# Two more chunks transposed by the DMA crossbar, and the chunk blocks chained earlier, in a retention + gated feed-forward kernel

## Chip, cores, metric

One core of a Trainium2 chip. The metric is device time in microseconds (us) of one execution. All executions compared here carry the label "fast" (the label leaves in a few that were somewhat disturbed, such as one execution of the kernel before with 236.82 us at a granted clock of 0.991). A ratio is the mean time of one kernel's fast runs over the mean of the other's in the same rounds, so it is not quite the ratio of the medians quoted beside it.

## The reference, cut to what matters

```python
# q, k, v: (4 batches, 8 heads, 768 positions, 64), fp32
for t in range(S):                                   # retention, per batch and head
    state = gamma * state + outer(k[t], v[t])
    y[t]  = q[t] @ state / sqrt(64)
x = y as (3072 tokens, 512)
out = (sigmoid(x @ w_gate) * (x @ w_val)) @ w_out    # d_ff 1536
```

## The kernel before

The kernel cuts each batch into six chunks of 128 positions: 24 chunks, in six tiles of 512 tokens (four chunks each). A tile's feed-forward ("up" groups, then "down" groups) is one long stream of matmuls. The retention work of later chunks is put between its groups by a plan: `(group, step, chunks)`. The helpers that the change touches:

```python
def transposes(g):                       # TensorE: 8 transposes, then a copy out of PSUM on ScalarE
    tp = bank([128, 2 * NP, C], BF16)
    for i, x in enumerate((kn[g], qn[g])):
        for p in range(NP):
            nc.tensor.transpose(tp[:, i * NP + p, :], pair(x, p), ident)
    qkT[g] = at.tile(...)
    nc.scalar.activation(qkT[g], tp, AX.Copy)

def xbar(g):                             # the same by the DMA crossbar, two transfers from SyncE
    qkT[g] = ld.tile(...)
    for i, x in enumerate((kn[g], qn[g])):
        nc.sync.dma_start_transpose(out=qkT[g][:, i * NP:(i + 1) * NP, :], in_=...)

def step_t(g):  transposes(g); scale_v(g)            # scale_v: one multiplication on VectorE

def block(done, new):                    # outputs of two old chunks, scores of two new ones
    # TensorE: inter(olds), scores(news), intra(olds), state(news)
    # VectorE: y_out(olds), [state_sum if no olds], masks(news), [state_sum if olds]

def casts(g):                            # ScalarE: two casts per chunk, state to bf16
    for i in range(g, g + 2): ... state_out(i, za[i])
```

Chunks 12 to 23 already go by the crossbar. Chunks 4 to 11 are transposed on TensorE. The first tile ("t = 0") starts with groups already done in a prologue.

## Time and profile before

| | before |
|---|---|
| median, 3 runs | 234.52 us (234.31 to 234.71) |
| span of the profiled run | 232.9 us |
| TensorE busy | 223.6 us, 96% |
| VectorE, ScalarE busy | 119.4 and 90.2 us |
| first "down" matmul of the first tile | 39.43 us |
| last TensorE work | 228.80 us |

I use three lengths, read from the chain of waits. The **head** runs up to the first down piece of the first tile. The **stream** runs from there to the end of TensorE's last piece. The **tail** runs from there to the end of the span. Before: 39.43, 189.37 and 4.10 us. Pieces of the chain of the kernel before (columns: start, length, engine, tile, line, count):

```profile
39.43 2.59 PE ff L418 x12
...
53.15 0.88 PE ff L384 x8
...
93.34 3.45 PE ff L384 x16
...
226.14 2.66 PE ff L437 x36
```

The second tile begins at 53.15 and the third at 93.34.

### The profile page before, as it was taken

What the parts mean: (1) busy time and instruction counts of PE and PEld (TensorE: products, weight loads), DVE (VectorE), ACT (ScalarE), POOL (GpSimd) and SP (SyncE); (2) the same over time, 40 slices, a digit from 0 to 9 for tenths busy, and PEclk for the clock granted to TensorE, in tenths of its full rate; (3) what the DMA queues carried; (4) which work ended last, traced back from release to release, by engine and by line L of the source; (5) the groups of instructions that cost most, each with busy time, mean ns of one, the idle gap of its engine ahead of it and who ended that gap; (6) DMA issues with size and microseconds to landing.
All of it is one profiled execution on the core that took longest, in us unless ns stands there. A gap on an engine that the chain in (4) does not pass through costs nothing.

```text
span 232.9 us, 4615 instructions
## 1 busy us (share of the span) xinstructions
PE 223.6 (96%) x1882; PEld 124.7 (54%) x1882; DVE 119.4 (51%) x228; ACT 90.2 (39%) x165; POOL 75.5 (32%) x98
## 2 busy tenths in 40 slices
PE   4889999999999999999999999999999999999992
PEld 1557844568889644445445445445445454444452
DVE  5579344175986544476835367637267530334201
ACT  5865333545837221362611532613532412343220
POOL 7997756999863619026000000000000000000000
PEclk9999999999999999999999999999999999999999
DMA  7999999999999999989111442012100012100022
GB/s 136 184 225 196 199 206 211 238 235 258 217 150 127 161 136 238 259 133 166 49 45 64 119 91 47 0 45 79 61 0 3 0 46 90 48 0 0 1 90 93
DMA packets 73302, 27.05 MB, mean 116 GB/s; under 512 B 59840, under 2 KB 68928, under 8 KB 73280
## 3 DMA queue, kind: packets, MB, share of 16 engines
q0 software_dynamic: 55440, 16.78, 64.8%
q1 hardware_dynamic: 17696, 9.90, 19.5%
q8 instruction: 15, 0.25, 0.4%
q10 hardware_dynamic: 144, 0.07, 0.1%
q14 instruction: 7, 0.06, 0.1%
HBM read 28.31 MB, written 6.29 MB: 149 GB/s over the span
## 4 chain that ended last, share of the span: by engine, by line
PE 87%; DMA 3%; POOL 3%; DVE 2%; issue 2%; ACT 1%; POOLq 0%
PE ff L384 43%; PE ff L418 25%; PE ff L400 8%; DMA qr<-in_q_dram 3%; PE ff L233 2%; PE ff L184 2%; PE ff L196 2%; PE ff L163 1%; PE ff L437 1%; PE z L202 1%; POOL kr L77 1%; DVE stA L189 1%; ACT gs L388 1%; ACT zbd L208 0%; DVE xT L251 0%
## 5 line engine op out<-in xcount | busy, mean ns | idle before, releaser
L389 DVE TENSOR_TENSOR hT<-gs,ff 128x512 bf16<-128x512 f32 (+1 forms) x66 | 42.1, 646 | 58.7 <-PE ff L384 53.7
L384 PE MATMUL ff<-xT,wg 128*128 128x512 bf16 (+1 forms) x264 | 63.6, 363 | 0.0
L384 PE MATMUL ff<-xT,wv 128*128 128x512 bf16 (+1 forms) x264 | 63.5, 363 | 0.0
L418 PE MATMUL ff<-wo,hT 128*128 128x512 bf16 x276 | 62.3, 379 | 0.2 <-DVE hT L389 0.2
L388 ACT ACTIVATE gs<-ff 128x512 f32<-128x512 f32 (+1 forms) x66 | 37.2, 566 | 64.6 <-PE ff L384 57.5
L418 PEld LDWEIGHTS <-hT 128*128 128x128 bf16 x276 | 26.3, 98 | 31.2 <-DVE hT L389 0.6
L384 PEld LDWEIGHTS <-wv 128*128 128x128 bf16 x264 | 25.9, 98 | 26.9
L384 PEld LDWEIGHTS <-wg 128*128 128x128 bf16 x264 | 25.0, 98 | 26.0 <-DVE xT L251 0.3
L423 ACT COPY ob<-ff 128x512 f32<-128x512 f32 x23 | 13.5, 587 | 48.8 <-PE ff L418 45.9
L251 DVE TENSOR_TENSOR xT<-ff,taby 128x512 bf16<-128x512 f32 x20 | 12.9, 686 | 21.0 <-PE ff L233 21.0
L67 POOL DMA_DIRECT2D kn<-in_k_dram x20 | 18.0, 901 | 15.3 <-DMA qkX<-qn 9.9
L62 POOL DMA_DIRECT2D vf<-in_v_dram x20 | 18.2, 912 | 12.0 <-DMA kn<-in_k_dram 5.4
L208 ACT CAST zbd<-za 64x256 bf16<-64x256 f32 x38 | 15.4, 405 | 9.5 <-DVE za L220 8.0
L68 POOL DMA_DIRECT2D qn<-in_q_dram x20 | 18.1, 903 | 2.9 <-DMA wo<-in_moe_w_out_dram 1.6
L175 DVE TENSOR_TENSOR vs<-vf,tabv 128x512 bf16<-128x512 f32 x20 | 13.5, 685 | 1.9 <-DMA vf<-in_v_dram 1.8
L189 DVE TENSOR_TENSOR stA<-ff,causal 128x512 bf16<-128x512 f32 x20 | 13.6, 682 | 0.0
L190 DVE TENSOR_TENSOR stB<-ff,causal 128x512 bf16<-128x512 f32 x20 | 13.6, 681 | 0.0
L400 PE MATMUL ff<-xT,wg 128*128 128x256 bf16 x88 | 11.6, 273 | 0.3 <-DVE xT L342 0.3
L400 PE MATMUL ff<-xT,wv 128*128 128x256 bf16 x88 | 11.6, 273 | 0.0
L407 DVE TENSOR_TENSOR hT<-gs,ff 128x512 bf16<-128x512 f32 x11 | 7.5, 687 | 7.3 <-PE ff L400 5.6
L400 PEld LDWEIGHTS <-wg 128*128 128x128 bf16 x88 | 8.4, 98 | 1.7 <-issue 0.6
L406 ACT ACTIVATE gs<-ff 128x512 f32<-128x512 f32 x11 | 6.5, 598 | 7.2 <-PE ff L400 7.2
(84 smaller groups left out, 160.6 us busy)
## 6 DMA issues: line engine op xcount, KB each, us to landing
out_dram<-ob SPq DMA_DIRECT2D x23, 256.0 KB, 2.0
vf<-in_v_dram POOLq DMA_DIRECT2D x20, 256.0 KB, 7.3
kn<-in_k_dram POOLq DMA_DIRECT2D x20, 128.0 KB, 7.3
qn<-in_q_dram POOLq DMA_DIRECT2D x20, 128.0 KB, 7.4
wg<-in_moe_w_gate_dram POOLq DMA_DIRECT2D x6, 256.0 KB, 8.9
wv<-in_moe_w_val_dram POOLq DMA_DIRECT2D x6, 256.0 KB, 9.4
wo<-in_moe_w_out_dram POOLq DMA_DIRECT2D x4, 384.0 KB, 11.3
vr<-in_v_dram SPq DMA_DIRECT2D x1, 512.0 KB, 4.3
```

The lines of the kernel that those rows point to most:

```text
L62: nc.gpsimd.dma_start(out=vf[g], in_=src(v, g))
L67: nc.gpsimd.dma_start(out=kn[g], in_=src(k, g))
L68: nc.gpsimd.dma_start(out=qn[g], in_=src(q, g))
L175: nc.vector.tensor_tensor(vs[g], vf[g], tabv[:, g % NCH, :].unsqueeze(2).to_broadcast([C, H, D]), op=ALU.mult)
L189: nc.vector.tensor_tensor(stA[g], sc[g][0], causal4, op=ALU.mult)
L190: nc.vector.tensor_tensor(stB[g], sc[g][1], causal4, op=ALU.mult)
L208: nc.scalar.copy(zbd[g % 4][half, :, half], z[half])
L384: nc.tensor.matmul(u[:, lo:hi], w[:, kk, n1 * 128:(n1 + 1) * 128], x_cols(t, kk, lo, hi), start=(kk == 0), stop=(kk == KT - 1))
L388: nc.scalar.activation(gs[:, lo:hi], ps[0][:, lo:hi], AX.Sigmoid)
L389: nc.vector.tensor_tensor(hT[t][:, n1, lo:hi], gs[:, lo:hi], ps[1][:, lo:hi], op=ALU.mult)
L400: nc.tensor.matmul(u[:, i * n:(i + 1) * n], w[:, kk, n1 * 128:(n1 + 1) * 128], x_cols(t, kk, lo, hi), start=(kk == 0 and (rows == 1 or i = ...
L418: nc.tensor.matmul(o, hT[t][:, n1, sm * 128:(sm + 1) * 128], wo[:, n1, :], start=(n1 == 0), stop=(n1 == NFF - 1))
```

## The change

Its intent: take the transposes of chunks 10 and 11 off TensorE. For that their crossbar transfers stand at the head of SyncE's work in the second tile. The retention blocks are chained and moved earlier, so that fewer half-wide up groups are needed. Two more output buffers are meant to keep ScalarE from waiting when stores stand behind crossbar transfers.

```diff
-    XBAR = 12
+    XBAR = 10
-        ob = ffn.tile([128, D_MODEL], F32, tag="ob", name="ob")
+        ob = ffn.tile([128, D_MODEL], F32, tag="ob", name="ob", bufs=5)
 plan:
-        0: [(7, step_t, 4), (9, step_t, 5), (10, block, None, 4), (10, casts, 4), (11, step_t, 6), (12, block, 4, None)],
-        1: [(0, step_t, 7), (2, block, None, 6), (3, step_t, 8), (4, casts, 6), (5, step_t, 9), (7, block, 6, 8),
-            (9, casts, 8), (11, step_t, 10), (13, step_t, 11), (15, block, 8, 10), (17, casts, 10), (20, block, 10, None),
-            (22, scale_v, 12), (23, scale_v, 13)],
-        2: [(1, block, None, 12), (3, casts, 12), ...
+        0: [(6, step_t, 4), (7, step_t, 5), (8, block, None, 4), (9, step_t, 6), (10, casts, 4), (10, step_t, 7),
+            (12, block, 4, 6), (13, step_t, 8)],
+        1: [(0, casts, 6), (1, step_t, 9), (3, block, 6, 8), (5, casts, 8), (7, scale_v, 10), (9, scale_v, 11),
+            (11, block, 8, 10), (13, casts, 10), (14, scale_v, 12), (15, scale_v, 13), (18, block, 10, 12),
+            (20, casts, 12)],
+        2: [(0, scale_v, 14), (1, scale_v, 15), (4, block, 12, 14), ...
 second tile, column halves:
-            groups[:10] = [... up(1, n1, 0, 256) for n1 in range(10)]
-            groups[10:10] = [... up_columns(1, range(n1, n1 + 2), 256, 512) for n1 in range(0, 10, 2)]
+            groups[:6] = [... up(1, n1, 0, 256) for n1 in range(6)]
+            groups[6:6] = [... up_columns(1, range(n1, n1 + 2), 256, 512) for n1 in range(0, 6, 2)]
 loop over groups:
+            if t == 1 and i == 0:
+                for g in range(XBAR, 12):
+                    xbar(g)
             if i == len(groups) - 9:
                 for g in range(4 * t + 8, 4 * t + 12):
-                    if XBAR <= g < NG:
+                    if 12 <= g < NG:
                         xbar(g)
```

More of the change, by code (lines that the diff above doesn't have):

```diff
@@ L531 @@
     plan = {
-        0: [(7, step_t, 4), (9, step_t, 5), (10, block, None, 4), (10, casts, 4), (11, step_t, 6), (12, block, 4, None)],
-        1: [(0, step_t, 7), (2, block, None, 6), (3, step_t, 8), (4, casts, 6), (5, step_t, 9), (7, block, 6, 8),
-            (9, casts, 8), (11, step_t, 10), (13, step_t, 11), (15, block, 8, 10), (17, casts, 10), (20, block, 10, None),
-            (22, scale_v, 12), (23, scale_v, 13)],
-        2: [(1, block, None, 12), (3, casts, 12), (4, scale_v, 14), (5, scale_v, 15), (7, block, 12, 14),
-            (9, casts, 14), (13, scale_v, 16), (14, scale_v, 17), (16, block, 14, 16), (18, casts, 16)],
+        0: [(6, step_t, 4), (7, step_t, 5), (8, block, None, 4), (9, step_t, 6), (10, casts, 4), (10, step_t, 7),
[3 more added lines that the diff above has]
+            (20, casts, 12)],
+        2: [(0, scale_v, 14), (1, scale_v, 15), (4, block, 12, 14), (6, casts, 14), (11, scale_v, 16),
+            (12, scale_v, 17), (16, block, 14, 16), (18, casts, 16)],
         3: [(3, scale_v, 18), (4, scale_v, 19), (6, block, 16, 18), (8, casts, 18), (12, scale_v, 20),
@@ L551 @@
         if t == 1:
-            groups[:10] = [lambda n1=n1: up(1, n1, 0, 256) for n1 in range(10)]
-            groups[10:10] = [lambda n1=n1: up_columns(1, range(n1, n1 + 2), 256, 512) for n1 in range(0, 10, 2)]
+            groups[:6] = [lambda n1=n1: up(1, n1, 0, 256) for n1 in range(6)]
+            groups[6:6] = [lambda n1=n1: up_columns(1, range(n1, n1 + 2), 256, 512) for n1 in range(0, 6, 2)]
             for g in range(12, 16):
```

## The prediction

> **What bounds the kernel now.** I read the page's busy table and slices first, then the chain of waits, then the timeline of the second tile (52.99 to 93.18 us), where the change works, and last the DMA issues there. The busy table and the slices come first because they tell which engine's time is the kernel's time:
>
> ```profile
> PE 223.6 (96%) x1882; PEld 124.7 (54%) x1882; DVE 119.4 (51%) x228; ACT 90.2 (39%) x165; POOL 75.5 (32%) x98
> ...
> PE   4889999999999999999999999999999999999992
> ...
> PEclk9999999999999999999999999999999999999999
> DMA  7999999999999999989111442012100012100022
> ```
>
> TensorE (PE) works in every slice after the third, at the full granted clock. VectorE (DVE) and ScalarE (ACT) are near half. The DMA engines are full until about slice 18 (some 105 us), then nearly idle. So the kernel is TensorE's own stream after the first 16.7 us, and a change pays what it takes off that stream or out of the small holes in it. The groups by shape say what is in it:
>
> ```profile
> L384 PE MATMUL ff<-xT,wg 128*128 128x512 bf16 x224 | 57.5, 379 | 0.0
> L384 PE MATMUL ff<-xT,wg 128*128 128x256 bf16 x40 | 6.0, 273 | 0.0
> L163 PE MATMUL ff<-ident,qn 128*128 128x128 bf16 x32 | 3.1, 219 | 0.0
> L163 PE MATMUL ff<-ident,kn 128*128 128x128 bf16 x32 | 3.1, 219 | 0.0
> ```
>
> The 219 ns of a transpose is its latency; what it costs is the pitch, read from the timeline and the chain: eight transposes advance the stream by 0.447 us, so 55.9 ns each; four matmuls 512 wide by 0.864 us, so 216.0 ns; four 256 wide by 0.437 us, so 109.3 ns. The chain of waits shows the second tile's holes, where it leaves TensorE for ScalarE:
>
> ```profile
> 58.13 0.46 PE ff L163 x8
> 58.59 0.02 issue
> 58.61 0.02 ACT qkT L165
> ...
> 59.53 0.38 ACT gs L388
> ...
> 61.90 0.60 ACT qkT L165
> ...
> 63.52 0.38 PE ff L184 x7
> ```
>
> ScalarE carries a 1.02 us copy out of PSUM for each transposed chunk, the sigmoids of half-wide groups, and four state casts of 0.4 us. Here they queue: TensorE waits at the block of chunks 6 to 9 for the copy of chunk 9.
>
> How large are the holes? The second tile takes 40.19 us between chain entries (53.15 to 93.34). Its work at the pitches above: 160 half-wide matmuls 17.49; 16 full ones of the up part 3.46; 48 of the down part at 215.7 ns 10.35; five transposed chunks 2.24; scores of six chunks at 0.275 each 1.65; states of five at 0.185, 0.92; inter of five at 0.224, 1.12; intra of six at 0.285, 1.71. Sum 38.94, so **1.25 us of holes**. The first tile's down stage by the same count has 0.22 us (two pieces of six matmuls take 1.40 instead of 1.29).
>
> [...]merging two 256-wide matmuls into one saves only some 2.6 ns. [...]a crossbar transpose lands in 2.4 us at 130 us, and in 8 to 10.6 us between 60 and 77 us among the loads. [...]the loads of chunk 17, issued at 69.6 and 70.4 us while transposes were queued, took 17.0 and 16.7 us, and those issued at 41 to 44 us beside no transpose took 5.9 to 6.4.
>
> **The change part by part.**
>
> 1. Transposes. Chunks 10 and 11 leave TensorE: 2 x 8 x 55.9 ns = **0.89 us** off the stream, all on the path. Also two copies of 1.02 us leave ScalarE, which costs nothing by itself.
>
> 2. Half-wide groups. Second-tile groups cut in column halves fall from 10 to 6. That turns 64 matmuls of 256 columns into 32 of 512: 64 x 109.3 - 32 x 216.0 = **0.08 us** saved.
>
> 3. Order. In the first tile the blocks are now chained (scores of chunks 6 and 7 in the same block as the outputs of 4 and 5), transposes of 7 and 8 move there from the second tile, and the block of 12 and 13 moves from the third tile to the end of the second. This moves work, and takes none away. Laying the order out at the trace's pitches, the second tile starts about 54.8 us instead of 52.99, with 1.8 us more done.
>
> 4. Holes after the change. First tile: the copies of chunks 4 to 7 fall among down matmuls, where ScalarE has one 0.59 us output copy per 2.6 us, so I expect near none (0.22 saved). Second tile: the casts of chunks 6 and 7 now wait for VectorE's sums, which stand behind two output multiplications (1.2 us) and four masks (2.4 us) of the chained block: about 57.0 us. The casts end near 58.3, then sigmoid, the copy of chunk 9 (to 59.6) and two sigmoids (to 60.4). TensorE reaches the block of 6 to 9 at about 58.9 and needs those: an estimated **1.3 us** of holes, the same size as the 1.25 before, moved. The hole of 0.15 us where the down stage waits for VectorE at 83.9 is inside that 1.25; three up groups now follow the block of 8 to 11 instead of two, so this one should go. Third tile, by the same count as above: 0.37 us of holes before, and I leave it. So holes before in the two tiles 1.47, after about 1.3: **0.15 us** saved.
>
> 5. Crossbar. The four new issues stand behind the first tile's fourth output (copied at about 55.0) and behind the loads of chunks 10 and 11, landed at 54.2, 55.7, 57.3 and 58.1 us. Four issues of 1.3 to 1.6 us from 55.4, landing 8 to 10 us later, spaced 2 us: the last about 70. The block that reads them starts near 73.5: margin **some 3 to 4 us**. Later transposes shift by about 4 us: chunk 13 from 75.4 to 79.5, wanted at about 86.5; chunk 15 from 86.8 to 91, wanted at about 102; the values of chunk 13 from 65.1 to 69, wanted at 81. All hidden.
>
> 6. Fifth output buffer. The first store of the second tile would be held in SyncE's order behind chunk 15's transposes, until about 82 us at my shift; its copy comes about 84. So it is an insurance, worth nothing if step 5 holds.
>
> Sum: 0.89 + 0.08 + 0.15 = 1.1 us. **Predicted 233.4 us**, 0.5% faster.
>
> **Rivals.** First: the crossbar lands too late. For it: the loads in that stretch already take 13 to 17 us when transposes are among them, and transposes among loads land up to 10.6 us after issue. Against: 3 to 4 us of margin. If the last transpose lands 3 us past its need, TensorE waits 3 us, less the gain of 1.1: 236 to 237 us. Second: the holes grow. [...]the chained block puts 4.4 us on VectorE in front of the casts; if each of the two chained blocks in the half-wide stretch costs 1 us more than I laid out, the gain is eaten: 234.5 to 235. Third: the holes close. If the chain of casts fits, all 1.47 us go as well as the 0.97 of removed work: 232.1. More can't be had, as everything else on the stream is unchanged, so the downside is longer than the upside.
>
> **Range and chances.** 232.2 to 235.0: the low end is nearly the third rival, the high end the second or a small form of the first. Two per cent is 4.7 us; faster by that is out of reach of the sum (2.5 us at most), so 0.01. Slower by it needs the first rival at 6 us of wait: 0.03. Within: 0.96.
>
> **What would show it.** Right: 16 fewer transposes on TensorE and 32 fewer matmuls; eight-transpose pieces unchanged at 0.45 us; the second tile starting near 54.8 and ending near 92; no wait of TensorE for a crossbar transpose; holes between 58.5 and 61 us with ScalarE in the chain. Wrong: TensorE waiting for the transposed chunk 10 or 11 at about 73 us (step 5), a lower total of holes by over 0.6 us (step 4), or a stall of the third tile on chunks 14 to 17, whose loads come later.

Passages that no trace of this case shows are cut from it where marked. No term of its sum is among them: 0.89 + 0.08 + 0.15 = 1.12 us, given as 1.1. The 215.7 ns of a down matmul is the trace's own: in the chain of the kernel before, 30 of them take 6.47 us. The 2.6 ns of a merge are 2 x 109.3 - 216.0 from its measured pitches.

## The result

231.88 us median (231.38 to 232.04, 4 runs). The kernel before had 234.42 us (233.78 to 234.71, 4 runs). The ratio is 0.9892, 95% interval 0.9866 to 0.9918. So the change is faster by 1.1%: "within 2%" as expected, but 1.5 us better than predicted and below the range of 232.2 to 235.0.

The page of the changed kernel, its busy table and slices:

```profile
PE 222.0 (97%) x1834; PEld 120.9 (53%) x1834; DVE 119.1 (52%) x226; ACT 88.1 (38%) x161; POOL 75.3 (33%) x98
...
PE   4989999999999999999999999999999999999994
...
DMA  7999999999999999999997342011100012100022
```

TensorE has 48 matmul instructions fewer (1882 to 1834): 16 transposes, and 64 narrow matmuls that became 32 wide ones. It still bounds the kernel. The DMA engines stay full some three slices longer. The groups of TensorE by shape, of the changed kernel:

```profile
L384 PE MATMUL ff<-xT,wg 128*128 128x512 bf16 x240 | 61.6, 379 | 0.0
...
L384 PE MATMUL ff<-xT,wg 128*128 128x256 bf16 x24 | 3.6, 273 | 0.0
...
L163 PE MATMUL ff<-ident,kn 128*128 128x128 bf16 x24 | 2.3, 219 | 0.0
L163 PE MATMUL ff<-ident,qn 128*128 128x128 bf16 x24 | 2.3, 219 | 0.0
```

The marks in its chain of waits:

```profile
38.63 1.29 PE ff L418 x6
...
54.05 1.75 PE ff L384 x16
...
92.30 8.63 PE ff L384 x40
...
224.07 2.66 PE ff L437 x36
```

Head 38.63, stream 226.73 - 38.63 = 188.10, tail 229.6 - 226.73 = 2.87. So the span fell by 3.3 us in this pair of profiles: 0.80 in the head, **1.27 in the stream**, 1.2 in the tail. My prediction had worked on the stream alone. There it said 1.1.

The hole that the prediction laid out in the second tile is there, at the place it named:

```profile
56.24 0.45 PE ff L384 x4
...
56.73 0.40 ACT zbd L208
...
57.15 0.41 ACT zbd L208
...
57.57 0.38 ACT gs L388
57.96 0.50 ACT qkT L165
...
58.76 0.68 ACT gs L388 x2
...
59.48 0.38 PE ff L184 x7
```

The chain leaves TensorE at 56.7, walks through the casts of chunks 6 and 7, a sigmoid, the copy of chunk 9 and two sigmoids, and returns at 59.5. The part of this in which TensorE lost time comes from the same count as before. The second tile takes 92.30 - 54.05 = 38.25 us. Its work at the prediction's pitches is 20.86 (96 half-wide and 48 full up matmuls) + 10.35 (down) + 0.45 (one transposed chunk) + 5.40 (scores, states, inter and intra) = 37.06. That leaves 1.19 us of holes.

Where did the head's and the tail's 2 us come from? The head holds no part of the change. In the tail, the landings of the last three stores differ. DMA issues after 226 us, kernel before (columns: transfer, queue, operation, count, KB, us from issue to landing):

```profile
q8 instruction: 1, 0.02, 0.6%
issues: line engine op xcount, KB each, median us to landing
out_dram<-ob SPq DMA_DIRECT2D x1, 256.0 KB, 4.2
out_dram<-ob SPq DMA_DIRECT2D x1, 128.0 KB, 3.3
out_dram<-ob ACTq DMA_DIRECT2D x1, 64.0 KB, 3.0
out_dram<-ob SPq DMA_DIRECT2D x1, 64.0 KB, 2.5
```

The same window of the changed kernel:

```profile
q14 instruction: 1, 0.01, 0.2%
...
out_dram<-ob SPq DMA_DIRECT2D x1, 128.0 KB, 1.7
out_dram<-ob ACTq DMA_DIRECT2D x1, 64.0 KB, 1.6
out_dram<-ob SPq DMA_DIRECT2D x1, 64.0 KB, 1.6
```

In the kernel before, one 16 KB packet of the queue q8 "instruction" stands beside the last stores. Its record runs from 228.08 to 229.41 us. In the changed kernel there is none (its q14 record is an 8 KB packet of another queue, and the landings are short beside it). Over the whole span the page counts 15 such packets before and 14 after. The listing of the built program has 3766 rows on TensorE before and 3670 after (each of the 1882 or 1834 matmuls has a weight load, and two rows are other instructions).

### The profile page after: what moved, and what is told of

The parts are those of the page before. It is cut to its first block, busy times and chain, and to the rows that moved or that the text cites. A ratio compares the mean times of both kernels' runs of the same rounds, so it can differ in the third digit from the quotient of the medians.

```text
span 229.6 us, 4530 instructions
## 1 busy us (share of the span) xinstructions
PE 222.0 (97%) x1834; PEld 120.9 (53%) x1834; DVE 119.1 (52%) x226; ACT 88.1 (38%) x161; POOL 75.3 (33%) x98
## 4 chain that ended last, share of the span: by engine, by line
PE 90%; POOL 3%; DMA 3%; ACT 1%; issue 1%; DVE 0%; POOLq 0%; ACTq 0%
PE ff L384 47%; PE ff L418 26%; PE ff L400 6%; DMA qr<-in_q_dram 3%; PE ff L233 2%; PE ff L184 2%; PE ff L196 2%; PE ff L163 1%; PE ff L437 1%; PE z L202 1%; POOL kr L77 1%; ACT gs L388 0%; POOL qr L77 0%; POOL vr L77 0%; POOL maskr L455 0%
## 5 line engine op out<-in xcount | busy, mean ns | idle before, releaser
L389 DVE TENSOR_TENSOR hT<-gs,ff 128x512 bf16<-128x512 f32 (+1 forms) x66 | 43.2, 662 | 58.9 <-PE ff L384 55.5
L384 PE MATMUL ff<-xT,wg 128*128 128x512 bf16 (+1 forms) x264 | 65.2, 369 | 0.0
L384 PE MATMUL ff<-xT,wv 128*128 128x512 bf16 (+1 forms) x264 | 65.2, 369 | 0.0
L388 ACT ACTIVATE gs<-ff 128x512 f32<-128x512 f32 (+1 forms) x66 | 38.0, 578 | 67.4 <-PE ff L384 61.4
L384 PEld LDWEIGHTS <-wg 128*128 128x128 bf16 x264 | 25.3, 98 | 27.5
L400 PE MATMUL ff<-xT,wg 128*128 128x256 bf16 x72 | 9.5, 273 | 0.3 <-DVE xT L342 0.3
L400 PE MATMUL ff<-xT,wv 128*128 128x256 bf16 x72 | 9.5, 273 | 0.0
L429 PE MATMUL ff<-ident 128*128 128x512 bf16 x18 | 6.3, 487 | 3.0 <-POOL ident masks.py:199 3.0
L407 DVE TENSOR_TENSOR hT<-gs,ff 128x512 bf16<-128x512 f32 x9 | 6.1, 684 | 5.0 <-PE ff L400 3.7
L406 ACT ACTIVATE gs<-ff 128x512 f32<-128x512 f32 x9 | 5.2, 596 | 6.5 <-PE ff L400 6.5
## 6 DMA issues: line engine op xcount, KB each, us to landing
kn<-in_k_dram POOLq DMA_DIRECT2D x20, 128.0 KB, 11.1
```

Of the source, the lines that this page charges most:

```text
L384: nc.tensor.matmul(u[:, lo:hi], w[:, kk, n1 * 128:(n1 + 1) * 128], x_cols(t, kk, lo, hi), start=(kk == 0), stop=(kk == KT - 1))
L388: nc.scalar.activation(gs[:, lo:hi], ps[0][:, lo:hi], AX.Sigmoid)
L389: nc.vector.tensor_tensor(hT[t][:, n1, lo:hi], gs[:, lo:hi], ps[1][:, lo:hi], op=ALU.mult)
L400: nc.tensor.matmul(u[:, i * n:(i + 1) * n], w[:, kk, n1 * 128:(n1 + 1) * 128], x_cols(t, kk, lo, hi), start=(kk == 0 and (rows == 1 or i = ...
```

## The experiments

All numbers of head, stream and tail are from each run's one profile (the span is read to 0.1 us, so a tail is good to about 0.05):

| run | rows on TensorE | head | stream | tail | median us | ratio to before (95%) |
|---|---|---|---|---|---|---|
| before (first profile) | 3766 | 39.43 | 189.37 | 4.10 | 234.42 | |
| after (first profile) | 3670 | 38.63 | 188.10 | 2.87 | 231.88 | 0.9892 (0.9866 to 0.9918) |
| before again | 3766 | 39.09 | 189.38 | 3.73 | 233.92 | 0.9979 (0.9953 to 1.0004) |
| after again | 3670 | 39.57 | 188.11 | 2.92 | 232.30 | 0.9910 (0.9876 to 0.9944) |
| order only | 3702 | 38.84 | 188.99 | 3.17 | 233.21 | 0.9956 (0.9926 to 0.9986) |
| crossbar only | 3734 | 39.16 | 188.49 | 2.85 | 232.23 | 0.9914 (0.9872 to 0.9955) |
| five buffers only | 3766 | 38.89 | 189.37 | 3.74 | 234.16 | 1.0013 (0.9951 to 1.0074) |
| after, rows added | 3766 | 39.40 | 188.11 | 3.99 | 232.88 | 0.9943 (0.9903 to 0.9984) |
| before, rows added | 3878 | 39.35 | 189.37 | 3.18 | 233.20 | 0.9956 (0.9915 to 0.9996) |
| after, three buffers | 3670 | 39.22 | 188.11 | 2.87 | 231.96 | 0.9902 (0.9853 to 0.9951) |
| split casts | 3670 | 38.99 | 187.25 | 2.86 | 231.02 | 0.9872 (0.9846 to 0.9899) |
| split casts, early sums | 3670 | 38.74 | 187.01 | 3.15 | 230.68 | 0.9854 (0.9825 to 0.9882) |

The stream repeats to 0.01 us for the same order of work. The head wanders between 38.6 and 39.6 us, as the two repeats show: 39.09 for before, 39.57 for after.

### The two kernels again

No edit.

> The kernel before, unchanged, as a control. In the two profiles the changed kernel gains 1.27 us between the first TensorE piece of the steady stream (16.72 before, 15.93 after) and the last (228.81, 226.73); 0.79 us more came before it (landing of the query load) and 1.2 us after it (landing of the last stores). Theory A, chance at the ends: this control's ratio is 1.000, but its own profile shows a start and a tail that differ from the first profile by several tenths of a us, and can show the short ones (start near 15.9, tail near 2.9 us). Theory B, the change shortens both ends: start stays near 16.7 and tail near 4.1 here.

> The changed kernel, unchanged. Theory A: ratio near (234.4-1.3)/234.4 = 0.9945 on the same chip, about 1.3 us, with start and tail no different from the control's. Theory B: ratio again near 0.989 (2.5 us), start near 15.9 and tail near 2.9.

Before gave 233.92 us and 0.9979. So 0.2% (0.5 us between the medians) is what the same kernel can differ from itself, and the intervals are to be read with that. After gave 232.30 us and 0.9910. Neither theory held as written. The streams repeat, 189.38 and 188.11. The head is chance: after had the longest head of all here. But the tail is not chance, with 3.73 again for before and 2.92 again for after.

### Order only

```diff
 changed kernel:
-    XBAR = 10
+    XBAR = 12
-            (7, scale_v, 10), (9, scale_v, 11),
+            (7, step_t, 10), (9, step_t, 11),
```

> The changed order, split and five buffers, but chunks 10 and 11 transposed on TensorE in the places of their scalings. If my sum is right (0.89 us of transposes, 0.08 of half-wide pairs, the rest in holes), this loses 0.9 us to the changed kernel plus what two extra copies on ScalarE cost in holes: 0.3 to 0.5 us faster than before, ratio about 0.998. If the order is what matters (rival), it keeps most of the gain: ratio 0.994 or below.

The stream is 188.99, so 0.38 us shorter than before, in the 0.3 to 0.5 expected. It loses 0.89 us to the changed kernel, which is 16 transposes at 55.9 ns. The total (0.9956, some 1.0 us) is larger than the stream explains. It lies between the 0.998 expected and the rival's 0.994, and its interval holds both, so by time alone neither was decided. The tail, at 3.17, is short here too.

### Crossbar only

```diff
 kernel before:
-    XBAR = 12
+    XBAR = 10
-            (11, step_t, 10), (13, step_t, 11),
+            (11, scale_v, 10), (13, scale_v, 11),
+            # at the head of the second tile: xbar(10), xbar(11); later crossbar steps from 12 on as before
-        ob = ffn.tile([128, D_MODEL], F32, tag="ob", name="ob")
+        ob = ffn.tile([128, D_MODEL], F32, tag="ob", name="ob", bufs=5)
```

> The order of before, with chunks 10 and 11 by the crossbar at the head of the second tile and five output buffers. If the transposes are the gain: 0.9 us faster, ratio about 0.996, same holes at the block of 6 to 9. If the crossbar needs the new order to land in time: TensorE waits at the block of chunks 8 to 11 (near 78 us) and the gain is smaller or lost; in that order the block is later (78 instead of 73), so I expect no wait.

The stream is 188.49, 0.88 us shorter, as expected. The ratio missed: 0.9914 where 0.996 was expected. By time alone this half can't be told from the whole change (0.9910 in the same rounds); only the streams separate them. No wait for the crossbar shows in the chain. The two parts add up: 0.38 + 0.88 = 1.26 us, the whole change's 1.27. The tail is 2.85, short again. So both halves of the change, which share no part of the plan, shorten the tail. They share two things: five output buffers, and a shorter instruction stream on TensorE.

### Five buffers only

```diff
 kernel before:
-        ob = ffn.tile([128, D_MODEL], F32, tag="ob", name="ob")
+        ob = ffn.tile([128, D_MODEL], F32, tag="ob", name="ob", bufs=5)
```

> The kernel before with five output buffers, nothing else. The profiles of before and of its repeat have a tail (last TensorE work to end of span) of 4.1 and 3.7 us, the three with the change or a part of it 2.85 to 3.2; these three also all have five buffers. Theory F (an instruction fetch of TensorE, [...]stands in the way of the last stores): TensorE's stream is as long as before (3766 program rows), so the fetch still comes at about 228 us, the tail stays 3.7 to 4.1, ratio 1.000. Theory G (the buffers shorten the tail): tail 2.9, ratio 0.996. The steady stream from the first down matmul to TensorE's last stays 189.4 us in both.

Tail 3.74, ratio 1.0013, and the 16 KB packet is again in the window of the last stores. The buffers are not the cause.

### The changed kernel with as many TensorE rows as before

```diff
+    def keep_on_split(parts, u):           # the same 512 columns in n pieces
+        for n in parts:
+            w = 128 * 4 // n
+            for j in range(n):
+                r, c = divmod(j * w, 128)
+                nc.tensor.matmul(u[:, r, c:c + w], ident, ident[:, c:c + w], start=True, stop=True)
-    keep_on(8, warm)
+    keep_on_split([8] * 6 + [4] * 2, warm)
```

> The changed kernel with 48 more matmuls in the warm-up before the data come (the same columns, cut smaller: no more array work), so that TensorE's stream has 3766 program rows as in the kernel before. Theory F: a fifteenth 16 KB fetch comes back beside the last stores, the tail is again 3.7 to 4.1 us, the stream stays 188.1 us, and the time is about 1 us above the changed kernel's: 233.0 to 233.3, ratio to before about 0.995. Theory G or chance: tail 2.9, ratio 0.990 to 0.991.

The issues after 226 us of this run:

```profile
q8 instruction: 1, 0.02, 0.4%
q14 instruction: 1, 0.01, 0.3%
...
out_dram<-ob SPq DMA_DIRECT2D x1, 128.0 KB, 3.5
out_dram<-ob ACTq DMA_DIRECT2D x1, 64.0 KB, 3.2
out_dram<-ob SPq DMA_DIRECT2D x1, 64.0 KB, 2.7
```

The fifteenth packet is back, the landings are long again, and the tail is 3.99 with an unchanged stream of 188.11. The time is 232.88 us, 0.9 us above the three-buffer variant of the changed kernel on the same chip (231.96). That one has the changed kernel's stream and tail. The expectation of 233.0 to 233.3 was missed by 0.1.

### The kernel before, with the fetch moved away from the end

```diff
 kernel before, with the helper above:
-    keep_on(8, warm)
+    keep_on_split([8] * 8, warm)
```

> The kernel before with 56 more matmuls in its warm-up (same columns, cut smaller): 3878 rows, so the last fetch comes some 112 rows, about 4 us, ahead of the end and clear of the last three stores. Theory F: tail near 2.9 us, stream 189.4 as before, about 1 us faster than before with nothing of the change in it, ratio about 0.996. Theory G: tail 3.7 to 4.1, ratio 1.000.

The record of the last 16 KB packet now runs from 216.75 to 218.11 us. It starts 11.3 us earlier than in the kernel before. The expectation had said about 4 us (as an estimate, 112 rows at the pace of the last piece, 72 rows in 2.66 us, are 4.1) and was wrong there, but the packet is clear of the last stores, as it should be. Their landings:

```profile
out_dram<-ob SPq DMA_DIRECT2D x1, 128.0 KB, 1.7
out_dram<-ob ACTq DMA_DIRECT2D x1, 64.0 KB, 1.7
out_dram<-ob SPq DMA_DIRECT2D x1, 64.0 KB, 1.6
```

The tail is 3.18, and the stream is still 189.37. The time is 233.20 us, ratio 0.9956: about 1 us, with nothing of the change in it. Together with the run before, this settles the tail. Adding instructions to the changed kernel brings the delay back, adding more to the old kernel takes it away, and both times the packet's place goes with it.

The traces also show how much of a store is late. The store that ScalarE issues (queue q10) is 144 packets. In the kernel before, 135 of them start between 229 and 230 us, and the rest only in the window from 230.5 to 231 us:

```profile
q10 hardware_dynamic: 9, 0.00, 2.8%
```

More than 0.95 us after TensorE's end, nine packets of this queue were still to come in the kernel before, in the run with rows added and in the run with five buffers, and eight in the repeat of before. In the changed kernel, its repeat and this run there were none. Nine of 144 is one sixteenth, so by an estimate from these counts the share of a single one of the 16 DMA engines is late, if the packets are spread evenly over them, which no trace here shows. The packet's own record is only 0.9 to 1.35 us long in the four profiles with it. Why these nine come up to 1.6 us after it has ended, no run here shows.

### The changed kernel with three buffers

```diff
-        ob = ffn.tile([128, D_MODEL], F32, tag="ob", name="ob", bufs=5)
+        ob = ffn.tile([128, D_MODEL], F32, tag="ob", name="ob", bufs=3)
```

> The changed kernel with three output buffers as before. My step 6: the buffers are insurance only; SyncE's last transpose of the second tile was issued at 81.3 us and the first store's copy ended at 83.2, so nothing waits: stream 188.1 us, tail 2.9, same time as the changed kernel. If the buffers matter, ScalarE's copies wait for stores at 83 to 93 us or the tail grows.

Stream 188.11, tail 2.87, 231.96 us. The two further buffers buy nothing here.

### Closing the hole that is left

```diff
 first run, changed kernel:
+    def cast(g):
+        state_out(g, za[g])
-        1: [(0, casts, 6), (1, step_t, 9), (3, block, 6, 8), (5, casts, 8), ...
+        1: [(0, cast, 6), (1, step_t, 9), (3, block, 6, 8), (4, cast, 7), (5, casts, 8), ...
 second run, in addition, in block():
-        if news and not olds:
+        early = not olds or new == 6
+        if news and early:
             state_sum(new)
         ...masks...
-        if news and olds:
+        if news and not early:
             state_sum(new)
```

> The changed kernel, aimed at the hole of 1.2 us that it still has at the block of chunks 6 to 9: the state cast of chunk 7, which that block doesn't read, moves behind the block; only the cast of chunk 6 stands in front of the sigmoids and the copy of chunk 9. If that queue on ScalarE is the hole, two casts of 0.41 us less in front close about 0.8 us: stream 187.3 us against 188.1, time near 231.2, ratio about 0.988. If the hole is VectorE's or PSUM's, nothing moves: 188.1.

> As the run before it, and VectorE forms the state sums of chunks 6 and 7 ahead of the four masks of their block instead of behind them, so the cast of chunk 6 starts about 2.4 us sooner. If the casts' start is what is left of the hole: stream near 187.0, ratio about 0.987. If the masks, now 0.8 us later, hold PSUM banks longer than TensorE can wait, a hole opens before the block and it is no better than the split alone, or worse.

Streams 187.25 and 187.01, as expected to 0.05 us, and 231.02 and 230.68 us. The stretch of the chain in the second run, which in the changed kernel left TensorE for ScalarE, no longer does:

```profile
56.35 1.75 PE ff L388 x16
58.10 0.22 PE ff L196 x4
58.33 0.55 PE ff L184 x16
```

The last run beats both kernels: 3.4 us below the kernel before on its chip (234.09), and its stream is 1.09 us shorter than the changed kernel's.

## Why the prediction was right or wrong

**Parts 1 and 2, the removed work**, held. The crossbar alone took 0.88 us off the stream, against 0.89 laid out. The order alone took 0.38, of which the merged halves are 0.08 by the same pitches.

**Part 3, the order**, held. The second tile was to start near 54.8 us with a head of 39.43. It started at 54.05 with a head of 38.63, which is 54.85 at equal heads. The end, "near 92", was a slip: 54.8 plus 37.06 of work (counted above) and 1.3 of holes is 93.2. At equal heads it ended at 93.10, as the sum says; that the trace reads 92.30 is the luck of a head that was 0.80 us shorter.

**Part 4, the holes**, held for the second tile to within about a tenth. Predicted were 1.3 us left in the second tile, through the casts of chunks 6 and 7, the copy of chunk 9 and the sigmoids; the trace has 1.19 and exactly that queue. That the queue was the cause is shown by the two last runs, which closed 1.09 us by moving casts and sums alone. I had counted 0.15 us of holes saved. The stream's 1.27, less 0.97 of removed work, makes it 0.30.

The 0.15 was put together wrongly, though. I had read 0.22 us of holes in the first tile off two pieces of 1.40 us. Both stand in the new chain too, so they were no waits for ScalarE, and none of this was saved. By the marks of the chain, 0.11 us was gained elsewhere in the first tile, 0.06 in the second and 0.11 in the third (whose 0.37 us of holes I get as 0.13 when I redo the count). This goes with two blocks fewer in these tiles, seven for nine: the piece after a block takes 0.1 us longer (1.40 instead of 1.29 for six matmuls), and the state matmuls of two chunks take 0.37 us in a block without outputs and 0.25 in a chained one. No run here tests that alone.

**Part 5, the crossbar**, held in its verdict but with less room than I gave it. The last of the four transfers was issued at 60.69 us and took 11.5, so it landed at 72.2; TensorE read it from 73.5. The margin was 1.3 us, not 3 to 4, because these four transfers, beside loads, took 8.3 to 11.5 us where I put 8 to 10. (Where no loads ran, around 130 us, a crossbar transfer landed in 2.4 us.) The loads are slower too: over the whole span the median landing of the key loads rose from 7.3 to 11.1 us with two more chunks transposed so (12.2 with the crossbar alone, 7.4 with the order alone).

**Part 6, the buffers**, held: insurance only, as the three-buffer run shows.

**The step that failed** is in the rivals and the range: "More can't be had, as everything else on the stream is unchanged". It rests on the first step, "a change pays what it takes off that stream or out of the small holes in it". The sentence is nearly true of the stream, and I let the stream stand for the time. The span also has a tail, and I never asked what set its 4.1 us, although the prediction read the DMA issues of other stretches. In the kernel before, a 16 KB instruction fetch of TensorE fell beside the last stores. The change took 96 rows from TensorE's program, and that fetch was no longer made. Nothing in the change aimed at this: for the change it was luck.

Over the four profiles with the packet at the end the tail has a mean of 3.89 us; over the eight without, 2.98. That is **0.9 us** that my sum had as zero. Stream and tail give 1.27 + 0.9 = 2.2 us. The measured differences of medians are 2.5, 2.2 and 2.2 us in the three sets of runs (first result, repeat, three buffers); against the control of its own rounds the repeat's is only 1.6. Stream and tail alone would have put the time at some 232.3 us, just inside my range. The 0.3 to 0.4 us that are left over in the first result are of the size by which the control differed from itself (0.2%, 0.5 us), and no run explains them further. The head's 0.8 us in the first pair of profiles was chance.

The rivals: the late crossbar did not come true, though only by 1.3 us. The grown holes did not come either. The closed holes came near in time, but for another reason: the holes were still there.

## What to carry to other kernels

Before predicting from the stream of the bounding engine, split the span into head, stream and tail, and ask of each what ends it. The tail is a handful of transfers, and one foreign packet beside them weighed as much here (0.9 us) as sixteen transposes. If a change alters how many instructions an engine has, look at where its instruction fetches fall before and after (here 15 packets of 16 KB for 3766 rows on TensorE, 14 for 3670). And a hole predicted through a queue on a third engine is worth a follow-up: name the entry that the waiting block doesn't need, and move it behind.
